# Casts of weights on VectorE during the attention, an early conversion dealt over more batches, and longer landing times for reloads in the planner

## The chip, the cores and the metric

One core of a Trainium2 chip runs the whole program. The metric is device time of one execution in microseconds; lower is better. The engines are PE (TensorE), ACT (ScalarE), DVE (VectorE), POOL (GpSimd) and SP (SyncE); SP and POOL issue the transfers.

## The reference

```python
scores = scale * np.matmul(q, k.transpose(0, 1, 3, 2)) - np.log(S)
attn = 1.0 / (1.0 + np.exp(-scores))          # sigmoid, no row sum
x = np.matmul(attn, v)                        # 4 batches x 12 heads, S 448, D 64
xn = x / np.sqrt(np.mean(x * x, -1) + 1e-06) * rms_g      # x: 1792 x 768
g, val = xn @ w_gate, xn @ w_val              # 768 -> 1536
y = (g / (1 + np.exp(-g)) * val) @ w_out      # 1536 -> 768
h = y @ w_in                                  # 768 -> 2048
out = (h - np.tanh(h)) @ w_out2               # 2048 -> 768
```

All of it is in float32 (x is first brought to 1792 rows of 768, the heads side by side).

## The kernel before

**Stages.** The attention runs over 4 batches, each of 6 pairs of heads: scores (L565, matmuls L576), sigmoids on ACT (L582, L583), the product with v (L596, matmuls L606), the copy of the result out of PSUM (pair_end, L613) and the sum of squares for the norm (x_end, L619: ACT squares in L621, DVE adds in L628). A batch's norm (L634) sums over channels on PE (L640), DVE reads these sums (L644), POOL takes the power (L646), and PE then writes over the same bank (whole_bank, L297), for which DVE must have read it. Then come the jobs: parts of w_gate ("Ag"), w_val ("Av"), w_out ("B"), w_in ("C") and the second w_out ("D"), each for two batches at a time, by schemes with seven products in place of eight (matmuls L881, L938) or plainly (L963). A product of float32 values is three passes over a high and a low part; a weight's high part is a cast (wt<-cv, L290) and its low part a difference (L371).

**Weights.** A raw piece is loaded by SP or POOL (load_raw, L334, L337; two slots). values32 (L353) makes float32 of it: a cast to zero (zero<-wt, L290) and a shift with an "or" on DVE (L360). For w_gate and w_val the conversion (conv, L436) goes on with sums (L452), splits, and stores to DRAM by SP (L434); for w_out (rows_early, L399) with sums (L420) and stores by POOL. 30 units of w_out's early conversion stand beside batches 0 and 1 of the attention, the loads and conversions of the first jobs of w_gate and w_val beside batch 3.

**Partial sums.** A job adds what it finished to sums kept in DRAM: POOL accumulates them (keep_sum, L748, L755). SP loads them again where a later job wants them: reload_sum (L675, L678) for the products with w_in, whose differences DVE takes in L691; reload_x (L670), prologue (L763) and set_units' get (L840) elsewhere. The epilogue's functions are L795 (silu), L798, L802 (tanh) and L803; additions of parts are L741 and L817.

**What sets the order.** Nothing runs while the code is read: each step is handed to a planner (Plan, L71) with the engines it may use and a modelled duration, what it reads and writes, and `after`, the modelled time from the end of an issue to the landing of a transfer (LAND; twice that for POOL). issue() takes, time after time, among the steps that could start within 300 ns of the soonest, the one of lowest rank (its place in the code plus `plan.later`), each on the engine that is done first, and at last writes out the program by modelled start. So a larger `after` puts what reads the data later and leaves the steps around it to move up. `copy` (L287) gives a cast or copy to ACT or DVE, whichever the planner finds sooner; with `act_copies` to ACT alone, which all jobs behind the attention have. `mixed` (L1050) deals lists of units evenly among the units of a batch's attention, with a rank some 60 places later. SP and POOL issue in the order of the program, and a waiting issue holds those behind it, as on every engine.

## Time and profile before

| | |
|---|---|
| Median of 3 runs | 1104.87 us (1102.76 to 1105.17) |
| The profiled execution | 1105.29 us |
| Span of its trace | 1103.5 us |
| Mean granted TensorE clock | 0.988 |
| PE busy | 1060.3 us (96%) |
| DVE, ACT, POOL busy | 773.2, 703.2, 138.8 us |

PE is busy nearly all the time, so the table says where little is left: in the stretches in which PE waits, and in those in which the throttle grants it less than the full clock. Where these are is read from the waits and the timelines. In a timeline row the bracket holds the idle time ahead of the instruction and what ended it; neighbours of one kind are one row with a count.

### The profile page before, as it was taken

Reading aid. Unit: us, or ns where it says so; the run is one execution under the profiler, and the core shown is the slowest. Engines: PE = TensorE matmul, PEld = TensorE weight load, DVE = VectorE, ACT = ScalarE, POOL = GpSimd, SP = SyncE. Lnnn points to the kernel's source line nnn. Section 1 sums busy time; section 2 is a strip of 40 time slices with the busy share of each in tenths; the row PEclk is TensorE's granted clock in tenths of the full one; section 3 lists DMA queues with packets and bytes.
Section 4 is the critical chain, followed back from the end, with each engine's and each line's share of the span. In section 5 each row is a group of like instructions: output and inputs, shape, how many; then the busy total and the mean of one; then the engine's idle time right before and its main releaser. Section 6 shows DMA issues by size and latency. Waiting matters only on the chain.

```text
span 1103.5 us, 15119 instructions
## 1 busy us (share of the span) xinstructions
PE 1060.3 (96%) x5148; PEld 877.4 (80%) x5148; DVE 773.2 (70%) x1212; ACT 703.2 (64%) x1263; POOL 138.8 (13%) x194
## 2 busy tenths in 40 slices
PE   8996999999999999999999799999999899999998
PEld 3332334999999889999999688989998789999997
DVE  3526571787687678786774585898886888677766
ACT  5763786567566546666666365686865776666652
POOL 2300000000003024111003012000303120003030
PEclk9997999999999999999999899999999999999999
DMA  8997454566866988969679639558958873649493
GB/s 311 343 336 225 129 145 159 189 230 202 310 209 172 313 301 161 333 235 314 237 259 270 187 87 226 188 192 306 225 193 212 248 177 107 201 158 209 121 190 125
DMA packets 105357, 240.92 MB, mean 218 GB/s; under 512 B 27072, under 2 KB 58304, under 8 KB 105280
## 3 DMA queue, kind: packets, MB, share of 16 engines
q1 hardware_dynamic: 81712, 174.91, 47.0%
q0 software_dynamic: 23264, 64.89, 24.3%
q8 instruction: 40, 0.66, 0.2%
q14 instruction: 37, 0.30, 0.1%
q10 hardware_dynamic: 304, 0.16, 0.1%
HBM read 149.08 MB, written 90.83 MB: 217 GB/s over the span
## 4 chain that ended last, share of the span: by engine, by line
PE 75%; issue 5%; DMA 5%; DVE 4%; POOL 2%; ACT 1%; SPq 0%; POOLq 0%; DVEq 0%; ACTq 0%
PE ps L938 39%; PE ps L881 23%; PE ps L963 4%; PE ps L606 4%; PE ps L576 4%; DMA wt<-in_w_out 2%; POOL out L755 2%; DMA unit<-sumB 1%; DVE wt L371 1%; DMA wAg<-cv 1%; ACT unit L290 1%; DVE unit L686 1%; ACT wt L290 1%; DVE unit L817 0%; DVE cv L360 0%
## 5 line engine op out<-in xcount | busy, mean ns | idle before, releaser
L938 PE MATMUL ps<-unit,wt 128*128 128x448 f32 x2520 | 525.7, 367 | 14.3 <-DVE unit L817 9.2
L938 PEld LDWEIGHTS ps<-unit,wt 128*128 128x128 f32 x2520 | 473.0, 188 | 60.4 <-DVE unit L817 10.8
L881 PE MATMUL ps<-unit,wt 128*128 128x448 f32 x1512 | 315.0, 366 | 3.4 <-DVE unit L686 1.5
L881 PEld LDWEIGHTS ps<-unit,wt 128*128 128x128 f32 x1512 | 283.3, 188 | 29.5 <-DVE unit L686 2.3
L371 DVE TENSOR_TENSOR wt<-cv,wt 128x768 fp32r<-128x768 f32 (+1 forms) x252 | 223.0, 891 | 99.8 <-ACT wt L290 97.8
L290 ACT COPY unit<-ps 128x448 f32<-128x448 f32 x297 | 156.2, 533 | 137.9 <-PE ps L938 54.4
L290 ACT CAST wt<-cv 128x768 fp32r<-128x768 f32 (+1 forms) x246 | 191.7, 784 | 79.1 <-PE ps L938 38.3
L290 ACT CAST unit<-unit 128x448 fp32r<-128x448 f32 x257 | 141.4, 567 | 49.8 <-DVE unit L798 19.7
L686 DVE TENSOR_TENSOR unit<-unit 128x448 fp32r<-128x448 f32 x252 | 152.4, 620 | 26.5 <-ACT unit L290 18.0
L817 DVE TENSOR_TENSOR unit<-ps,unit 128x448 f32<-128x448 f32 x168 | 103.6, 621 | 33.9 <-PE ps L938 20.8
L691 DVE TENSOR_TENSOR unit<-unit 128x448 f32<-128x448 f32 x144 | 88.1, 620 | 24.3 <-DMA unit<-sumB 18.2
L576 PE MATMUL ps<-wt 64*128 64x448 f32 (+1 forms) x384 | 82.7, 559 | 15.0 <-ACT unit L583 11.9
L583 ACT ACTIVATE unit<-ps 128x448 f32<-128x448 f32 (+1 forms) x192 | 86.1, 547 | 9.3 <-PE ps L576 9.3
L576 PEld LDWEIGHTS ps<-wt 64*128 64x128 f32 (+1 forms) x384 | 33.4, 176 | 60.5 <-issue 41.4
L606 PE MATMUL ps<-unit,cv 128*64 128x448 f32 (+1 forms) x384 | 79.3, 554 | 2.1 <-DMA cv<-in_vp 2.1
L360 DVE SCALAR_TENSOR_TENSOR cv<-wt,zero 128x768 uint32<-128x768 uint32 x68 | 64.9, 954 | 19.7 <-ACT zero L290 14.9
L290 ACT CAST zero<-wt 128x768 f16<-128x768 bf16 x56 | 60.2, 1075 | 21.5 <-DMA wt<-in_w_val 12.2
L755 POOL DMA_DIRECT2D sumB<-unit x48 | 41.4, 947 | 247.3 <-DVE unit L817 155.8
L606 PEld LDWEIGHTS ps<-unit,cv 128*64 128x64 f32 (+1 forms) x384 | 26.0, 139 | 52.3 <-issue 33.2
L963 PE MATMUL ps<-unit,wt 128*128 128x448 f32 x288 | 62.4, 374 | 2.8 <-ACT unit L290 1.9
L963 PEld LDWEIGHTS ps<-unit,wt 128*128 128x128 f32 x288 | 54.8, 192 | 9.4 <-ACT unit L290 2.7
L755 POOL DMA_DIRECT2D out<-unit x36 | 30.9, 937 | 180.5 <-DVE unit L817 164.1
(45 smaller groups left out, 402.3 us busy)
## 6 DMA issues: line engine op xcount, KB each, us to landing
wt<-in_w_out POOLq DMA_DIRECT2D x28, 768.0 KB, 7.9
cv<-wD SPq DMA_DIRECT2D x56, 384.0 KB, 5.4
cv<-wB SPq DMA_DIRECT2D x36, 384.0 KB, 5.5
wt<-in_w_in SPq DMA_DIRECT2D x16, 768.0 KB, 6.5
wC<-cv SPq DMA_DIRECT2D x32, 384.0 KB, 5.3
cv<-wC SPq DMA_DIRECT2D x32, 384.0 KB, 5.6
sumB<-unit POOLq DMA_DIRECT2D x48, 224.0 KB, 7.1
wD<-cv POOLq DMA_DIRECT2D x28, 384.0 KB, 6.1
```

Source lines behind the costliest of these rows:

```text
L290: add(engines, lambda e: (nc.scalar.copy if e == "ACT" else nc.vector.tensor_copy)(to(), of()), reads, writes)
L371: add({**dve(n, psum=False), **pool(n)}, lambda e: ENG[e].tensor_sub(lo(), of(), hi().bitcast(F32)), [*reads, *kh], [*kl])
L576: nc.tensor.matmul(ps[i, c].tile[:n, :S], lhsT=t.tile[rows, at:at + n], rhs=t.tile[rows, :S], start=True, stop=True)
L583: add(act(S, psum=True), lambda e: nc.scalar.activation(to.tile[at:at + n, :S], ps.tile[:n, :S], AF.Sigmoid, bias=-math.log(S), scale=1.0 ...
L606: nc.tensor.matmul(ps.tile[i * D:(i + 1) * D, :S], lhsT=v.tile[:n, c, i, :], rhs=a[c][i].tile[:n, :], start=(c == 0), stop=(c == 3))
L686: add({**pool(S), **dve(S, psum=False)}, lambda e: ENG[e].tensor_sub(t["l"].tile, of.tile, t["h"].tile.bitcast(F32)), [of["t"], kh], [kl])
L691: add({**dve(S, psum=False), **pool(S)}, lambda e: ENG[e].tensor_sub(t.tile, x.tile, y.tile), [x["t"], y["t"]], [t["t"]])
L755: add({"POOL": (1100, False)}, lambda e: nc.gpsimd.dma_start(out=d.tile, in_=t.tile, accum_op=ALU.add), [t["t"], d["t"]], [d["t"]], after= ...
L817: add(dve(S), lambda e: nc.vector.tensor_add(t.tile, ps.tile[:, :S], t.tile), [ps["t"], t["t"]], [t["t"]])
L881: nc.tensor.matmul(ps.tile[:, :S], lhsT=part(a), rhs=x[b].tile, start=n in (1, 5) and kp == 0 and q == 0, stop=kp == n_kp - 1 and q == 2, ...
L938: nc.tensor.matmul(ps.tile[:, :S], lhsT=part(a), rhs=x[b].tile, start=n in ((1, 2, 5) if opening else (1, 5)) and i == 0 and q == 0, stop= ...
L963: nc.tensor.matmul(ps.tile[:, :S], lhsT=wt, rhs=a[p].tile, start=start and i == 0, stop=stop and i == 2, skip_group_check=True)
```

## The change

It has three parts. `act_copies` becomes `copies_by`, which names an engine or none: the units of the early conversion of w_out, and those of the first two jobs' conversion beside batch 3, are wrapped by `by_dve`, so that their casts are DVE's; the copies of the attention itself stay free, and all jobs behind it have ACT as before. The 30 units of w_out are dealt 6, 12, 12 and 0 over the four batches where they were dealt 8 and 22 over the first two. And the planner counts 4500 ns to the landing of a load where it counted 3500 (POOL's: 9000 for 7000), and 10000 for the four kinds of reloads.

```diff
@@ -26,7 +26,6 @@
 SG = 4
 SPLIT = []
 EARLY = {"Ag": 0, "Av": 0, "C": 0}
-ACT_COPIES = "AgAvBCD"
 PLAIN_SETS = {("B", 0): (2,), ("D", 0): (), ("B", 1): (2,), ("D", 1): ()}
 
 NQK = S + 4 * P
@@ -42,9 +41,10 @@
 BEHIND, ROWS_BEHIND = 90, 90
 FIRST = 150
 HELD = 3
+ROWS_B = 20, 60, 100
 ROWS_BY = {"B": "POOL", "D": "POOL"}
 N_AGAIN = 4
-LAND = 3500
+LAND, FAR = 4500, 10000
 WINDOW = 500
 N_UNIT, N_MOE, N_RAW, N_WT, N_CV = 72, 40, 2, 8, 8
 AHEAD = 2
@@ -79,7 +79,7 @@
 
     def __init__(self, room):
         self.room, self.work, self.rank, self.later = room, [], [], 0
-        self.act_copies = False
+        self.copies_by = None
 
     def add(self, engines, run, reads=(), writes=(), stream=None, after=0):
 
@@ -285,8 +285,8 @@
         return {}
 
     def copy(engines, to, of, reads, writes):
-        if plan.act_copies:
-            engines = {"ACT": engines["ACT"]}
+        if plan.copies_by:
+            engines = {plan.copies_by: engines[plan.copies_by]}
         add(engines, lambda e: (nc.scalar.copy if e == "ACT" else nc.vector.tensor_copy)(to(), of()), reads, writes)
 
     g_sb = const.tile([P, KM], F32, name="g_sb")
@@ -670,12 +670,12 @@
     def reload_x(b, c):
         x = xs[b, c] = unit("xr")
         d = spilled.pop((b, c))
-        add({"SP": (650, False)}, lambda e: nc.sync.dma_start(out=x.tile, in_=d.tile), [d["t"]], [x[0], x[1]], after=LAND)
+        add({"SP": (650, False)}, lambda e: nc.sync.dma_start(out=x.tile, in_=d.tile), [d["t"]], [x[0], x[1]], after=FAR)
 
     def reload_sum(b, c):
         x = xg[b, c] = unit("xr")
         d = sums_t.pop(("B", b, c))
-        add({"SP": (650, False)}, lambda e: nc.sync.dma_start(out=x.tile, in_=d.tile), [d["t"]], [x["t"]], after=LAND)
+        add({"SP": (650, False)}, lambda e: nc.sync.dma_start(out=x.tile, in_=d.tile), [d["t"]], [x["t"]], after=FAR)
 
     right = {}
 
@@ -765,7 +765,7 @@
             ps = ps_t[ph, b, m] = bank("m2")
             if carried(ph, bs, s):
                 d, a = sums_t.pop((ph, b, m)), unit("accs")
-                add({"SP": (650, False)}, lambda e, a=a, d=d: nc.sync.dma_start(out=a.tile, in_=d.tile), [d["t"]], [a["t"]], after=LAND)
+                add({"SP": (650, False)}, lambda e, a=a, d=d: nc.sync.dma_start(out=a.tile, in_=d.tile), [d["t"]], [a["t"]], after=FAR)
                 seed(ps, a, False)
 
     def seed(to, of, psum):
@@ -841,7 +841,7 @@
             for mp in range(KM // 2):
                 a, d = unit("accs"), sums_t.pop((ph, bs[n], 2 * mp + m))
                 accs[m, n, mp] = a
-                add({"SP": (650, False)}, lambda e, a=a, d=d: nc.sync.dma_start(out=a.tile, in_=d.tile), [d["t"]], [a["t"]], after=LAND)
+                add({"SP": (650, False)}, lambda e, a=a, d=d: nc.sync.dma_start(out=a.tile, in_=d.tile), [d["t"]], [a["t"]], after=FAR)
 
         def done(n, mp):
             x, y, z = (banks.get((c, mp)) for c in "xyz")
@@ -1047,6 +1047,14 @@
                 units += part
         return units
 
+    def by_dve(units):
+        def run(u):
+            plan.copies_by = "DVE"
+            u()
+            plan.copies_by = None
+
+        return [lambda u=u: run(u) for u in units]
+
     def mixed(units, *others):
 
 
@@ -1063,13 +1071,14 @@
                     plan.later = 0
                     at[k] += 1
 
-    rows_b = [u for i in range(n_sets("B")) for u in rows_early("B", i)]
-    mixed(attn_units(0), rows_b[:8])
-    mixed(attn_units(1), [lambda: norm(0), lambda: spread_norm(0)], rows_b[8:])
-    mixed(attn_units(2), [lambda: norm(1), lambda: spread_norm(1), *x_units("A", BATCHES[0], False)])
+    rows_b = by_dve([u for i in range(n_sets("B")) for u in rows_early("B", i)])
+    at = [len(rows_b) * x // 100 for x in ROWS_B]
+    mixed(attn_units(0), rows_b[:at[0]])
+    mixed(attn_units(1), [lambda: norm(0), lambda: spread_norm(0)], rows_b[at[0]:at[1]])
+    mixed(attn_units(2), [lambda: norm(1), lambda: spread_norm(1), *x_units("A", BATCHES[0], False)], rows_b[at[1]:at[2]])
     for j in range(AHEAD):
         load(j)
-    mixed(attn_units(3), [lambda: norm(2)], [u for j in range(AHEAD) for u in (*conv(j), lambda j=j: load(j + AHEAD))])
+    mixed(attn_units(3), [lambda: norm(2)], [u for j in range(AHEAD) for u in (*by_dve(conv(j)), lambda j=j: load(j + AHEAD))], rows_b[at[2]:])
     norm(3)
 
 
@@ -1092,7 +1101,7 @@
 
     for j in range(len(jobs)):
         ahead = conv(j + AHEAD) + [lambda: load(j + 2 * AHEAD)]
-        plan.act_copies = jobs[j][0] in ACT_COPIES
+        plan.copies_by = "ACT"
         kind = kind_of(j)
         tight = is_tight(j)
         units = job_units(j, tight)
```

The order of the instructions shows the following. In names, a number tells one buffer from the next.

At the end of batch 1 SP issues loads of queries and keys (in_qkt), of values (in_vp, in_vt) and of raw weights. Before:

```order
L337 DMA wt_650<-in_w_gate 128x3072
L547 DMA cv_677<-in_vp 128x384
L547 DMA cv_677<-in_vp 32x128
L547 DMA cv_677<-in_vp 64x64 x2
L337 DMA wt_697<-in_w_gate 128x3072
L537 DMA wt_713<-in_qkt 128x896
L337 DMA wt_726<-in_w_val 128x3072
L434 DMA wAg_0_746<-cv_728 128x768
L547 DMA cv_759<-in_vp 128x384
L547 DMA cv_759<-in_vp 32x128
L547 DMA cv_759<-in_vp 64x64 x2
L537 DMA wt_780<-in_qkt 128x896
```

After:

```order
L547 DMA cv_674<-in_vp 128x384
L547 DMA cv_674<-in_vp 32x128
L547 DMA cv_674<-in_vp 64x64 x2
L537 DMA wt_698<-in_qkt 128x896
L337 DMA wt_702<-in_w_gate 128x3072
L547 DMA cv_722<-in_vp 128x384
L547 DMA cv_722<-in_vp 32x128
L547 DMA cv_722<-in_vp 64x64 x2
L537 DMA wt_745<-in_qkt 128x896
L337 DMA wt_749<-in_w_gate 128x3072
L337 DMA wt_775<-in_w_val 128x3072
```

Each load of w_gate now stands behind one or two loads of the attention more, and no store of a converted weight (wAg) stands between them; the next one comes behind the loads of in_vt.

On DVE at the same place, where wt_726 and wt_791 are raw pieces of w_val and L644 reads batch 0's norm. Before:

```order
L290 CAST zero_80<-wt_726 128x768
L360 SCALAR_TENSOR_TENSOR cv_829<-wt_726,zero_80 128x768
L290 CAST wt_843<-cv_728 128x768
L371 TENSOR_TENSOR wt_843<-cv_728,wt_843 128x768
L628 TENSOR_TENSOR unit_647<-unit_647,unit_846 128x448
L360 SCALAR_TENSOR_TENSOR cv_860<-wt_791,zero_80 128x768
L644 TENSOR_SCALAR ms_877<-ps_852 112x4
```

After, where wt_749 is the second raw piece of w_gate:

```order
L290 CAST zero_80<-wt_749 128x768
L360 SCALAR_TENSOR_TENSOR cv_831<-wt_749,zero_80 128x768
L628 TENSOR_TENSOR unit_632<-unit_632,unit_829 128x448
L452 TENSOR_TENSOR cv_850<-cv_831 128x3x128
L452 TENSOR_TENSOR cv_850<-cv_850,cv_796 128x3x128
L290 CAST wt_862<-cv_850 128x768
L371 TENSOR_TENSOR wt_862<-cv_850,wt_862 128x768
L644 TENSOR_SCALAR ms_879<-ps_855 112x4
```

Before, the cast of wt_791 (to zero) was ACT's and stood there among the sigmoids. Now all casts are DVE's, and L644 stands behind the whole conversion of w_gate's second piece, while w_val's come behind it.

On PE the norm itself moved by one group of matmuls. Before:

```order
L576 MATMUL ps<-wt 96x448 x4
L640 MATMUL ps<-ones,unit 112x1 x4
L576 MATMUL ps<-wt 128x448 x4
L297 LDWEIGHTS mark
L297 MATMUL ps<-mark 128x448
L606 MATMUL ps<-unit,cv 64x448 x8
L576 MATMUL ps<-wt 96x448 x4
```

After:

```order
L576 MATMUL ps<-wt 96x448 x4
L576 MATMUL ps<-wt 128x448 x4
L640 MATMUL ps<-ones,unit 112x1 x4
L606 MATMUL ps<-unit,cv 64x448 x8
L297 LDWEIGHTS mark
L297 MATMUL ps<-mark 128x448
L576 MATMUL ps<-wt 96x448 x4
```

L297, which writes the bank that L644 reads, now comes behind eight matmuls of L606 (sixteen in the trace's count) and not ahead of them.

Near 600 us DVE takes differences of reloaded sums (L691), and finishes products (L798, L817). Before:

```order
L691 TENSOR_TENSOR unit_5804<-unit_5761,unit_5754 128x448
L691 TENSOR_TENSOR unit_5816<-unit_5775,unit_5804 128x448
L371 TENSOR_TENSOR wt_5814<-cv_5625,wt_5814 128x768
L798 TENSOR_TENSOR unit_5451<-ps_5756,unit_5451 128x448
L371 TENSOR_TENSOR wt_5825<-cv_5702,wt_5825 128x384
L817 TENSOR_TENSOR unit_5809<-ps_5771,unit_5809 128x448
L741 TENSOR_TENSOR unit_5848<-unit_5451,unit_5837 128x448
L798 TENSOR_TENSOR unit_5480<-unit_5809,unit_5480 128x448
L817 TENSOR_TENSOR unit_5794<-ps_5739,unit_5794 128x448
```

After:

```order
L691 TENSOR_TENSOR unit_5817<-unit_5717,unit_5710 128x448
L798 TENSOR_TENSOR unit_5442<-ps_5759,unit_5442 128x448
L371 TENSOR_TENSOR wt_5812<-cv_5676,wt_5812 128x768
L741 TENSOR_TENSOR unit_5834<-unit_5442,unit_5829 128x448
L371 TENSOR_TENSOR wt_5822<-cv_5686,wt_5822 128x384
L817 TENSOR_TENSOR unit_5805<-ps_5772,unit_5805 128x448
L798 TENSOR_TENSOR unit_5474<-unit_5805,unit_5474 128x448
L817 TENSOR_TENSOR unit_5790<-ps_5742,unit_5790 128x448
```

One L691 is left ahead of L798 and L817; the other three come eight rows behind the last row shown. On SP the reloads of the first two sums come ahead of one load of w_in and one store that stood ahead of them.

At the end of the attention, ACT's order after (before, the first silu and its table load stand behind the last sigmoid):

```order
L583 ACTIVATE unit_1777<-ps_1750 128x448
L795 ACT_TABLE_LOAD
L795 ACTIVATE unit_1781<-unit_1681 128x448
L290 COPY unit_1795<-ps_1758 128x448
L621 ACTIVATE unit_1798<-unit_1795 128x448
L290 CAST zero_80<-wt_1664 128x768
L583 ACT_TABLE_LOAD
L583 ACTIVATE unit_1811<-ps_1783 96x448
L583 ACTIVATE unit_1815<-ps_1784 96x448
L583 ACTIVATE unit_1820<-ps_1785 96x448
```

One silu (L795) stands between two groups of sigmoids (L583), and with it two more table loads.


## Rows read from the trace of the kernel before

**Rows 1.** waits of TensorE, whole span: total us, times, longest

```profile
PE ps L576 <- ACT unit L583: 11.9, 2, 10.7
PE ps L938 <- DVE unit L817: 9.2, 3, 7.4
PE ps L963 <- ACT unit L290: 1.9, 2, 1.5
```

**Rows 2.** timeline of TensorE, attention: start, duration, instruction, [idle before <- releaser]

```profile
64.68 3.23 PE L606 MATMUL ps<-unit,cv 128*64 128x448 f32 x16 [2.14 <-DMA cv<-in_vp]
...
80.52 1.75 PE L576 MATMUL ps<-wt 64*96 64x448 f32 x8
...
95.50 1.86 PE L576 MATMUL ps<-wt 64*128 64x448 f32 x2 [10.65 <-ACT unit L583]
...
97.77 4.79 PE L606 MATMUL ps<-unit,cv 128*64 128x448 f32 x16
...
105.67 3.23 PE L606 MATMUL ps<-unit,cv 128*64 128x448 f32 x16
```

**Rows 3.** timeline of ScalarE, the same stretch

```profile
94.00 1.05 ACT L290 CAST zero<-wt 128x768 f16<-128x768 bf16 x1 [12.19 <-DMA wt<-in_w_val]
```

**Rows 4.** timeline of VectorE, the same stretch

```profile
80.60 0.60 DVE L290 CAST zero<-wt 128x768 f16<-128x768 bf16 x1 [13.35 <-DMA wt<-in_w_gate]
81.09 0.61 DVE L628 TENSOR_TENSOR unit<-unit 128x448 f32<-128x448 f32 x1
81.62 0.96 DVE L360 SCALAR_TENSOR_TENSOR cv<-wt,zero 128x768 uint32<-128x768 uint32 x1
82.62 0.56 DVE L290 CAST wt<-cv 128x768 fp32r<-128x768 f32 x1
83.21 0.96 DVE L371 TENSOR_TENSOR wt<-cv,wt 128x768 fp32r<-128x768 f32 x1
...
85.76 1.15 DVE L452 TENSOR_TENSOR cv<-cv 128x384 f32<-128x384 f32 x2
```

**Rows 5.** timeline of the queue of SyncE (SPq), the same stretch

```profile
73.45 0.52 SPq L337 DMA_DIRECT2D wt<-in_w_gate  x1
74.08 2.06 SPq L547 DMA_DIRECT2D cv<-in_vp  x4
...
85.48 0.53 SPq L537 DMA_DIRECT2D wt<-in_qkt  x1
86.11 0.38 SPq L337 DMA_DIRECT2D wt<-in_w_val  x1
```

**Rows 6.** landing times of the tile wt's transfers, 0 to 130 us

```profile
DMA to landing us min/median/max: 3.1/7.5/12.5
```

**Rows 7.** timeline of VectorE around 615 us

```profile
611.78 0.62 DVE L691 TENSOR_TENSOR unit<-unit 128x448 f32<-128x448 f32 x1 [8.14 <-DMA unit<-sumB]
614.95 0.63 DVE L691 TENSOR_TENSOR unit<-unit 128x448 f32<-128x448 f32 x1 [2.54 <-DMA unit<-sumB]
```

**Rows 8.** timeline of TensorE at 620 us; row of the chain at 959 us

```profile
619.63 25.75 PE L938 MATMUL ps<-unit,wt 128*128 128x448 f32 x117 [7.40 <-DVE unit L817]
...
959.24 21.90 PE ps L938 x108
```

**Rows 9.** SyncE's reloads near 600 us; their landing times, 560 to 680 us

```profile
597.50 3.01 SPq L678 DMA_DIRECT2D unit<-sumB  x4
...
DMA to landing us min/median/max: 2.8/8.4/14.7
```

**Rows 10.** windows: stretch; PE, PEld, DVE, ACT, POOL busy; PEclk, DMA share, GB/s

```profile
75.00:100.00 25.00, 14.35 (x61) 5.49 (x59) 15.79 (x28) 9.89 (x21) 1.03 (x1) 0.75 0.82 271
...
615.00:620.00 5.00, 0.37 (x1) 0.37 (x2) 4.97 (x9) 1.49 (x3) 0.00 (x0) 0.64 0.56 176
```

**Rows 11.** timeline of ScalarE at the end of the attention

```profile
195.60 1.28 ACT L795 ACT_TABLE_LOAD   x1
196.90 1.20 ACT L795 ACTIVATE unit<-unit 128x448 f32<-128x448 f32 x2
```

## The prediction

> **What bounds the kernel now.** I read the waits of TensorE first, then its timeline at the two longest, then the engines and the queue that those waits name. TensorE is busy for 96% of the span, so only its idle time and its time at a low clock can be won. Two waits stand out: 10.7 us of scores (L576) behind a sigmoid (L583), and 7.4 us of L938 behind an addition on VectorE (L817) [rows 1].
>
> The first is at the end of batch 1's attention. TensorE stops at 95.50 − 10.65 = 84.85 us [rows 2]. The sigmoids that should free its banks stand on ScalarE behind a cast that waits 12.19 us for a raw piece of w_val [rows 3]; SyncE issued that load at 86.11 [rows 5] and the cast could start at 94.00, so issue to use took 7.9 us. When TensorE resumes it is slow: two scores of L576 take 1.86 us [rows 2] where eight took 1.75, so 2 × 1.75 / 8 = 0.44 was due; the next sixteen L606 take 4.79 where others take 3.23. Together 1.42 + 1.56 = 3.0 us are lost; the window around it shows a granted clock of 0.75 [rows 10], a mix of the 1.2 and 2.4 GHz levels. This place costs 10.65 + 3.0 = **13.65 us**.
>
> The second is at 612 to 620 us. VectorE waits 8.14 and 2.54 us in L691 for reloaded sums [rows 7] that SyncE issued from 597.50 on and of which the slowest took 14.7 us to land [rows 9]; L817 stands behind them on VectorE, and TensorE idles 7.40 us [rows 8]. The 117 matmuls after that take 25.75 us, where 117 × 21.90 / 108 = 23.7 were due, so 2.0 go to the clock (0.64 granted in that window [rows 10]). It costs **9.4 us**.
>
> **The change part by part.** *The casts go to VectorE.* In the attention four casts to zero and two to wt change engine, 4 × 0.60 + 2 × 0.56 = 3.5 us more on VectorE [rows 4]. VectorE is busy 15.79 of the 25 us there [rows 10], so the time itself is hidden; uncovered it would be 3.5. ScalarE no longer holds a cast that waits for a weight until the attention's tail, so the 12.19 us wait leaves the sigmoids' queue. What is late next is on VectorE: L644 reads the norm's sums, TensorE's L297 writes over that bank afterwards, and in the new order L644 stands behind the whole conversion of the second w_gate piece. A waiting cast there holds L628, L452, L371 and L644, and then TensorE.
>
> When does that piece land? In the new order SyncE has, from the place of 73.45 us on [rows 5], a load of values (2.06), one of queries (0.53), the first w_gate (0.52), values again and queries again, before the second w_gate: 2.06 + 0.53 + 0.52 + 2.06 + 0.53 = 5.7, issue at 79.2. The store that waited for VectorE no longer stands ahead of it. The first w_gate piece went from issue at 73.45 [rows 5] to its cast at 80.60 [rows 4] in 7.15; so I put the second at 86.4. VectorE then does cast 0.60, L360 0.96, L628 0.61, two L452 1.15, cast 0.56, L371 0.96 [rows 4], 4.84 in all, and L644 runs at 91.2. TensorE, not stopped at 84.85, has the last two scores (0.44) and sixteen L606 (3.23) before L297 and reaches it at 88.5. Gap: 91.2 − 88.5 = 2.7.
>
> What does that gap cost in clock? Behind the idle time of 2.14 at 64.68 the sixteen L606 took 3.23 as elsewhere [rows 2], so nothing; behind 7.40 it was 2.0 [rows 8]. On the line between, 2.7 costs (2.7 − 2.14) / (7.40 − 2.14) × 2.0 = 0.2. So 13.65 becomes 2.9: **gain 10.7**. Bounds: 13.65, where the piece lands 2.7 us sooner and no gap is left; and 0, where the gap is again what it was. I take the value from the rows of this very load.
>
> *Loads of values.* With the weight loads behind them, the wait of 2.14 us for values at 64.68 [rows 2] may shrink: **gain 1**, between 0 and 2.14.
>
> *The early conversion of w_out.* 30 units go 6, 12, 12 beside batches 0 to 2 instead of 8 and 22 beside batches 0 and 1. That is only a rank for the planner, and the order shows little of it: the twelfth conversion stands on VectorE behind seven additions of squares (L628) where it stood behind five, some ten us later,, and is still in batch 1. POOL issues the same loads and stores. Its price is within the bounds above: **0**; if a store came to stand behind a later conversion, it would delay nothing before w_out is used, hundreds of us on.
>
> *Reloads planned 10 us long, other loads 4.5.* Near 600 us the sums' reloads move ahead on SyncE past one weight load and one store, and on VectorE three of the four L691 go some fifteen rows down; one L691 remains ahead of L798 and L817. If it starts with the first landing, as now at 611.78, its successors no longer wait for the second: L817 comes at least 614.95 − 611.78 = 3.2 earlier [rows 7]. The reloads' issue comes perhaps 4 us earlier too (one load and one store less, and the first pair first). With 3.2 + 4 the idle time of 7.40 is nearly gone, and its clock loss with it, in part. **Gain 7**, between 3.2 (landing unchanged) and 9.4 (all). Behind it the three L691 are next; the product that needs them comes later by these fifteen rows, and I count nothing.
>
> *The planner's other shifts.* From 360 to 410 us POOL issues four raws of the second w_out in a row instead of two and two. L963 waits 1.9 us in all for ScalarE [rows 1]. I take 0, from −2 to +4 (a queue of raws ahead of a store can delay what waits for it; of the two ends the first is the nearer).
>
> *Tables.* A silu (L795) now stands between two groups of sigmoids, so two more table loads: one took 1.28 [rows 11]. ScalarE has slack there and the matmuls of L938 now mixed between the last pairs fill TensorE: **cost 0.5**, between 0 and 2.6. The Trainium skill (ScalarE: Activation LUTs, What ACT_TABLE_LOAD costs) gives about 2.66 us per switch, since it adds a drain; here the next function starts at 196.90, right behind 195.60 + 1.28, so the trace shows no such drain.
>
> **Sum.** The profiled execution took 1105.29 us: its span of 1103.5 and 1.8 around it, and 0.4 over the median of 1104.87. 10.7 + 1 + 7 + 0 − 0.5 = 18.2, so 1105.3 − 18.2 = 1087.1, and 1086.7 on the median's side. Since the first term has more room below than above, I round up: **1088**.
>
> **The rivals.** *The wait only changes engines.* If the second w_gate lands after the longest of the loads, 12.5 us [rows 6], it is there at 91.7, L644 at 96.5, and the gap is 8.0 with (8.0 − 2.14) / 5.26 × 2.0 = 2.2 of clock: 10.2 of 13.65 remain, and the gain is 3.4. The time: 1105.3 − (3.4 + 1 + 7 − 0.5) = 1094.4, **1094**. For it: the DMA share of that window is 0.82 [rows 10]. Against: the piece before needed 7.15.
>
> *The sums land no earlier.* The DMA engines were full there, as 14.7 us to land say [rows 9]; an earlier issue may not help, and the waits pass to the three later L691. The third term is then 0 to 3.2: 1105.3 − (10.7 + 1 + 1.6 − 0.5) = 1092.5, **1093** (with the middle, 1.6).
>
> *Slower: the head of VectorE's queue.* The second w_gate is issued only behind the queries of 85.48 [rows 5], since SyncE must wait for free slots, and lands 12.5 later, at 98.0. L644 is at 102.8, the gap 14.3, and with clock 3.0 × 14.3 / 10.65 = 4.0 the place costs 18.3, 4.7 more than now. If the reloads gain nothing as well and the tables cost 0.5, it is 1105.3 + 5.2 = 1110.5, **1110**. It decides where the landing passes some 94 us with no gain at 612, or 100 with the whole of it.
>
> *The tables stand on TensorE's path.* Both loads would delay sigmoids that TensorE waits for: 2 × 1.28 = 2.56 instead of 0.5, **1090**. Against: they lie where L938 has work. By the Trainium skill's 2.66 (the same section) an estimate would be 5.3 instead of 2.56, 1093, with the rule that functions be grouped by table set; the trace's 1.28 bears out the lower.
>
> *The change does not do what it says.* The spread of w_out over three batches is such a case already; it carries no term, and is no rival in time.
>
> **How the numbers follow.** The forecast 0.58, the moved wait 0.17, the late sums 0.12, the slower one 0.08, the tables 0.05. Two runs of this kernel can be told apart by about 0.2%, 2.2 us. Faster by more than that: all of the forecast and the tables, 0.13 of the moved wait, 0.11 of the late sums, 0.87 in all. Within it: the rest of these two, where both shrink together, 0.05. Slower: 0.08. Range: from 1078, where both gaps vanish, the values come in time and the other shifts give their 2 (13.65 + 9.4 + 2.1 + 2 = 27.2), to 1102, where the moved wait and the late sums come together (3.4 + 1 − 0.5 = 3.9 is 1101.4).
>
> **What would show it.** Right: no sigmoid waits for a weight before 110 us; TensorE's idle time at L297 or the scores near 88 us is 1 to 5 us, with L644 behind a cast that waits for in_w_gate; L691 at 605 to 612 with one wait, and less than 3 us of idle time before L938 there. Wrong: L644 later than 95 us, an L691 wait of 8 us or more that TensorE repeats, or a new wait in the 200 to 1100 us that neither view above has. The forecast fails above all if SyncE's issues are held by slots, or if transfers land much later than 7 us.

## The result, and the profile after

The changed kernel takes 1089.2 us (median of 4 runs, 1087.35 to 1090.19) where the kernel before took 1104.0 in the same comparison: a ratio of 0.9864, 95% interval 0.9845 to 0.9883. The prediction was 1088 in a range of 1078 to 1102. The profiled execution, the fastest of the four, took 1087.35 with a span of 1085.6, so 17.9 us less span than before.

The waits of TensorE after (total us, times, longest) answer to [rows 1]:

```profile
PE ps L576 <- DMA wt<-in_qkt: 7.1, 2, 3.7
PE ps L938 <- ACT unit L290: 3.6, 3, 1.7
PE ps L297 <- DVE ms L644: 2.9, 1, 2.9
PE ps L938 <- DVE unit L817: 2.4, 3, 1.1
```

The 10.7 us behind the sigmoid and the 7.4 behind L817 are gone. In their place stand 2.9 us at L297 behind L644, which was forecast, and more for queries and keys at the very start, 7.1 us where it was 3.1 (2.69 and 0.41), which was not. TensorE's timeline of the attention answers to [rows 2]:

```profile
13.14 1.77 PE L576 MATMUL ps<-wt 64*128 64x448 f32 x8 [3.41 <-DMA wt<-in_qkt]
...
29.80 3.36 PE L576 MATMUL ps<-wt 64*128 64x448 f32 x8 [3.71 <-DMA wt<-in_qkt]
33.09 4.40 PE L606 MATMUL ps<-unit,cv 128*64 128x448 f32 x16
...
91.99 0.35 PE L297 MATMUL ps<-mark 128*128 128x448 bf16 x1 [2.90 <-DVE ms L644]
92.27 3.25 PE L576 MATMUL ps<-wt 64*96 64x448 f32 x16
95.45 3.23 PE L606 MATMUL ps<-unit,cv 128*64 128x448 f32 x16
```

VectorE, answering to [rows 4], shows what L644 waited for, and SyncE's queue, answering to [rows 5], when it was issued:

```profile
82.53 0.61 DVE L290 CAST zero<-wt 128x768 f16<-128x768 bf16 x1 [4.26 <-DMA wt<-in_w_gate]
...
87.02 0.62 DVE L290 CAST zero<-wt 128x768 f16<-128x768 bf16 x1 [1.19 <-DMA wt<-in_w_gate]
...
90.91 0.96 DVE L371 TENSOR_TENSOR wt<-cv,wt 128x768 fp32r<-128x768 f32 x1
91.79 0.15 DVE L644 TENSOR_SCALAR ms<-ps 112x4 f32<-112x4 f32 x1
```

```profile
75.91 0.51 SPq L337 DMA_DIRECT2D wt<-in_w_gate  x1
...
80.17 0.43 SPq L337 DMA_DIRECT2D wt<-in_w_gate  x1
```

VectorE's timeline near 590 us and then TensorE's, answering to [rows 7] and [rows 8]:

```profile
593.23 0.63 DVE L691 TENSOR_TENSOR unit<-unit 128x448 f32<-128x448 f32 x1 [7.63 <-DMA unit<-sumB]
```

```profile
597.75 3.97 PE L938 MATMUL ps<-unit,wt 128*128 128x448 f32 x18 [1.60 <-ACT unit L290]
602.22 24.00 PE L938 MATMUL ps<-unit,wt 128*128 128x448 f32 x117 [0.50 <-DVE unit L817]
```

One L691 still waits 7.63 us, but the second and the pair behind it no longer do, and TensorE loses 2.1 us where it lost 7.40. The 117 matmuls then take 24.00 us, not 25.75.

Where the 17.9 us came from can be read by the starts of the same TensorE instructions in both timelines:

| From one mark to the next (start in us before / after) | Gain in this stretch |
|---|---|
| start to the tenth group of sixteen L606 (77.36 / 78.64) | −1.3 |
| to the twelfth (105.67 / 95.45) | +11.5 |
| to the first 108 L881 (255.68 / 246.95) | −1.5 |
| to the second (332.71 / 323.87) | +0.1 |
| to 100 L963 (407.99 / 396.98) | +2.2 |
| to the next 108 L881 (498.56 / 486.00) | +1.55 |
| to the next (575.44 / 563.11) | −0.2 |
| to 100 L963 (654.84 / 635.67) | +6.8 |
| to two L881 (732.40 / 712.88) | +0.35 |
| to 86 L881 (1082.21 / 1064.17) | −1.5 |
| to the end of the span (1103.5 / 1085.6) | −0.1 |

### The profile page after: what moved, and what is told of

Its sections match the earlier page's. It is cut to its first block, busy times and chain, and to the rows that moved or that the text cites. A ratio compares the mean times of both kernels' runs of the same rounds, so it can differ in the third digit from the quotient of the medians.

```text
span 1085.6 us, 15124 instructions
## 1 busy us (share of the span) xinstructions
PE 1056.8 (97%) x5148; PEld 874.8 (81%) x5148; DVE 775.4 (71%) x1217; ACT 702.7 (65%) x1260; POOL 139.4 (13%) x194
## 4 chain that ended last, share of the span: by engine, by line
PE 73%; issue 10%; DMA 8%; DVE 3%; SPq 2%; POOL 2%; ACT 1%; POOLq 0%; DVEq 0%; ACTq 0%
PE ps L938 38%; PE ps L881 21%; PE ps L963 5%; PE ps L606 4%; PE ps L576 4%; DMA wt<-in_qkt 3%; POOL out L755 2%; DMA cv<-in_vp 2%; SPq L547 1%; DMA wt<-in_w_in 1%; DMA wt<-in_w_out 1%; DVE wt L371 1%; DMA out<-unit 1%; DVE unit L817 0%; DVE unit L686 0%
## 5 line engine op out<-in xcount | busy, mean ns | idle before, releaser
L938 PE MATMUL ps<-unit,wt 128*128 128x448 f32 x2520 | 524.8, 366 | 7.5 <-ACT unit L290 3.6
L938 PEld LDWEIGHTS ps<-unit,wt 128*128 128x128 f32 x2520 | 471.2, 188 | 56.1 <-ACT unit L290 6.4
L881 PE MATMUL ps<-unit,wt 128*128 128x448 f32 x1512 | 316.3, 367 | 4.0 <-DVE unit L686 1.6
L881 PEld LDWEIGHTS ps<-unit,wt 128*128 128x128 f32 x1512 | 284.8, 189 | 29.8 <-DVE unit L686 2.2
L290 ACT COPY unit<-ps 128x448 f32<-128x448 f32 x299 | 158.0, 534 | 138.9 <-PE ps L938 45.6
L290 ACT CAST wt<-cv 128x768 fp32r<-128x768 f32 (+1 forms) x244 | 190.3, 785 | 75.2 <-PE ps L938 32.0
L290 ACT CAST unit<-unit 128x448 fp32r<-128x448 f32 x256 | 140.9, 567 | 31.6 <-DVE unit L798 8.6
L817 DVE TENSOR_TENSOR unit<-ps,unit 128x448 f32<-128x448 f32 x168 | 103.5, 621 | 34.5 <-PE ps L938 17.1
L691 DVE TENSOR_TENSOR unit<-unit 128x448 f32<-128x448 f32 x144 | 87.7, 619 | 20.2 <-DMA unit<-sumB 14.0
L583 ACT ACTIVATE unit<-ps 128x448 f32<-128x448 f32 (+1 forms) x192 | 87.0, 546 | 18.7 <-PE ps L576 18.7
L576 PE MATMUL ps<-wt 64*128 64x448 f32 (+1 forms) x384 | 81.5, 558 | 7.1 <-DMA wt<-in_qkt 7.1
L606 PE MATMUL ps<-unit,cv 128*64 128x448 f32 (+1 forms) x384 | 79.1, 552 | 0.0
L576 PEld LDWEIGHTS ps<-wt 64*128 64x128 f32 (+1 forms) x384 | 32.6, 176 | 54.1 <-issue 47.5
L606 PEld LDWEIGHTS ps<-unit,cv 128*64 128x64 f32 (+1 forms) x384 | 25.6, 138 | 49.6 <-issue 32.4
L963 PE MATMUL ps<-unit,wt 128*128 128x448 f32 x288 | 60.9, 368 | 1.8 <-ACT unit L290 1.0
L290 ACT CAST zero<-wt 128x768 f16<-128x768 bf16 x52 | 56.0, 1076 | 9.9 <-DMA wt<-in_w_in 5.1
L963 PEld LDWEIGHTS ps<-unit,wt 128*128 128x128 f32 x288 | 53.6, 188 | 8.1 <-ACT unit L290 1.8
```

What stands on the lines that cost most here:

```text
L290: add(engines, lambda e: (nc.scalar.copy if e == "ACT" else nc.vector.tensor_copy)(to(), of()), reads, writes)
L576: nc.tensor.matmul(ps[i, c].tile[:n, :S], lhsT=t.tile[rows, at:at + n], rhs=t.tile[rows, :S], start=True, stop=True)
L583: add(act(S, psum=True), lambda e: nc.scalar.activation(to.tile[at:at + n, :S], ps.tile[:n, :S], AF.Sigmoid, bias=-math.log(S), scale=1.0 ...
L606: nc.tensor.matmul(ps.tile[i * D:(i + 1) * D, :S], lhsT=v.tile[:n, c, i, :], rhs=a[c][i].tile[:n, :], start=(c == 0), stop=(c == 3))
L691: add({**dve(S, psum=False), **pool(S)}, lambda e: ENG[e].tensor_sub(t.tile, x.tile, y.tile), [x["t"], y["t"]], [t["t"]])
L817: add(dve(S), lambda e: nc.vector.tensor_add(t.tile, ps.tile[:, :S], t.tile), [ps["t"], t["t"]], [t["t"]])
```

## The experiments

The first theory was the one of the prediction: the first place, at the end of batch 1, needs the casts on VectorE and SyncE's new order together; the second, near 600 us, is cured by the reloads' planned landing time. The rivals: the casts alone, or the planner's landing time for ordinary loads alone. All diffs below are against the changed kernel, if not said otherwise. With `ROWS_B = 27, 100, 100` the dealing is the old one (8 and 22 of 30 units), with 3500 the landing times are.

### One part at a time

**casts_only**

```diff
-ROWS_B = 20, 60, 100
+ROWS_B = 27, 100, 100
-LAND, FAR = 4500, 10000
+LAND, FAR = 3500, 3500
```

> Only the casts of the early conversions go to VectorE; the dealing (8, 22) and the planner's landing times (3500) are those of before. Theory 1 (the first place is cured by two things together: the cast must leave ScalarE, and SyncE must issue the w_gate loads ahead of the store that waits for VectorE): SyncE's order stays that of before, L644 stands on VectorE behind a cast of w_val whose load is issued near 86 us, so TensorE waits at L297 from about 85 to about 95 us; the second place is as before; 1101 to 1105 us. Theory 2 (taking the casts from ScalarE is enough for the first place): no wait over 4 us near 90 us; 1092 to 1095 us.

Measured: 1102.69 us, ratio to the kernel before 0.9987 (0.9966 to 1.0007), no difference that can be told. The wait only changed engines. TensorE, then VectorE:

```profile
92.17 0.53 PE L297 MATMUL ps<-mark 128*128 128x448 bf16 x1 [6.87 <-DVE ms L644]
```

```profile
78.82 0.62 DVE L290 CAST zero<-wt 128x768 f16<-128x768 bf16 x1 [10.53 <-DMA wt<-in_w_gate]
...
91.97 0.15 DVE L644 TENSOR_SCALAR ms<-ps 112x4 f32<-112x4 f32 x1
```

From 78.82 on VectorE never idles: L644 comes behind the conversions of three pieces and a cast of the fourth. So once the first piece of w_gate has landed it is work on VectorE that is waited for, and not the load of w_val, as the expectation had it.

**land_only**

```diff
-ROWS_B = 20, 60, 100
+ROWS_B = 27, 100, 100
-LAND, FAR = 4500, 10000
+LAND, FAR = 4500, 3500
-    rows_b = by_dve([u for i in range(n_sets("B")) for u in rows_early("B", i)])
+    rows_b = [u for i in range(n_sets("B")) for u in rows_early("B", i)]
...
-    ... (*by_dve(conv(j)), lambda j=j: load(j + AHEAD))], rows_b[at[2]:])
+    ... (*conv(j), lambda j=j: load(j + AHEAD))], rows_b[at[2]:])
```

> Only the modelled landing time of ordinary loads goes from 3500 to 4500 ns (reloads stay at 3500, casts are free, dealing 8 and 22). Its order on SyncE at the end of batch 1 and on VectorE near 600 us is that of the changed kernel. Theory 1: the cast of w_gate's or w_val's piece is still ScalarE's and holds the sigmoids, so 3 to 6 us of the first place remain, the second is cured by the order of L691: 1093 to 1097 us. Theory 2 (casts): the first place stays whole, 1097 to 1100. Theory 3 (the landing time alone makes the whole gain): 1087 to 1091 us.

Measured: 1092.83 us, ratio 0.9895 (0.9867 to 0.9922): 11.5 us, the largest of the single parts, and at the edge of what theory 1 expected. ScalarE's cast still waits, and TensorE too. The L290 that its row names is pair_end's copy, which VectorE had got and which came there, at 86.80, behind the conversion of another piece. ScalarE, then TensorE:

```profile
87.23 1.05 ACT L290 CAST zero<-wt 128x768 f16<-128x768 bf16 x1 [9.02 <-DMA wt<-in_w_gate]
```

```profile
87.47 3.58 PE L576 MATMUL ps<-wt 64*128 64x448 f32 x4 [4.08 <-DVE unit L290]
```

The second place is cured too: no wait behind L817 over 0.9 us is left, though one of 2.35 behind ScalarE has come.

**far_only** has `LAND, FAR = 3500, 10000`, with the old dealing and free casts as in land_only.

> Only the modelled landing time of the reloads goes from 3500 to 10000 ns. All four L691 near 600 us come behind L798 and L817; SyncE's order at the end of batch 1 is that of before. Theories 1 and 2: the second place is cured and the first stays, 1095 to 1098 us, with TensorE's wait of some 10 us near 95 us and none over 2 us near 612. Theory 3: the later L691 only hand the wait on, 1102 to 1105.

Measured: 1096.22 us, ratio 0.9917 (0.9888 to 0.9946). The first place is not cured. The second is, and wholly: the 171 L938 there run without a wait. TensorE at both places, then SyncE:

```profile
89.57 1.86 PE L576 MATMUL ps<-wt 64*128 64x448 f32 x2 [8.83 <-ACT unit L583]
...
593.67 34.88 PE L938 MATMUL ps<-unit,wt 128*128 128x448 f32 x171
```

```profile
590.14 3.01 SPq L678 DMA_DIRECT2D unit<-sumB  x4
```

The reloads were issued no earlier than before: 590.14 is 22.2 us behind the start of the 108 L881 ahead of them (567.92), where the kernel before had 22.1 (597.50 and 575.44). So L691's place behind L817 on VectorE is enough for the second place.

**deal_only** has the new dealing, 3500 for both landing times and free casts.

> Only the dealing of the early conversion of w_out changes (6, 12, 12 beside batches 0 to 2 for 8, 22). All theories: SyncE's order at the end of batch 1 and VectorE's near 600 us are those of before, so both places stay: 1102 to 1106 us. If the first 40 us have the wait of the changed kernel there (3.7 us and a low clock behind it), the dealing is its cause and the time is 1 to 4 us above before.

Measured: 1104.6 us, ratio 1.0009 (0.9990 to 1.0028). By itself the dealing does nothing to the time, as predicted. But it moves the norm on TensorE by one group of matmuls, as in the changed kernel (L640 behind sixteen L576, L297 behind the L606), and the wait of the first place now stands ahead of L640. The profile names no releaser; by the times it is again ScalarE's cast of w_val, with the sigmoids behind it. TensorE, then ScalarE:

```profile
93.02 1.62 PE L640 MATMUL ps<-ones,unit 128*112 128x1 f32 x8 [8.03 <-issue]
```

```profile
91.48 1.05 ACT L290 CAST zero<-wt 128x768 f16<-128x768 bf16 x1 [8.45 <-DMA wt<-in_w_val]
```

Its profile has 7.5 us of waits for queries at the start, casts_only 3.9, land_only 2.1 and far_only 1.7.

### All but one part

**all_but_casts** has free casts (the last two pieces of land_only's diff).

> The changed kernel with free casts in the attention (dealing and landing times as changed). SyncE's order is the changed one and L644 stands behind the same two L371 as in the changed kernel, while ScalarE has a cast to zero of a w_gate piece again. Theory 1 (place and cast both needed at the first place): 2 to 4 us slower than the changed kernel, 1091 to 1093, with a wait of sigmoids behind that cast. Theory 3 (the landing times make the gain, the engine of the casts matters only with the old order): within 2 us of the changed kernel, 1088 to 1091.

Measured: 1095.47 us, ratio to the kernel before 0.9906 (0.9881 to 0.9931): by the ratios some 5 us slower than the changed kernel (0.9906 against 0.9864; the intervals just touch), more than either theory gave. ScalarE's cast, then TensorE:

```profile
89.05 1.05 ACT L290 CAST zero<-wt 128x768 f16<-128x768 bf16 x1 [9.46 <-DMA wt<-in_w_gate]
```

```profile
89.26 1.86 PE L576 MATMUL ps<-wt 64*128 64x448 f32 x2 [4.82 <-DVE unit L290]
...
92.66 5.83 PE L606 MATMUL ps<-unit,cv 128*64 128x448 f32 x16
```

The cast holds ScalarE's sigmoids and, on VectorE, a copy out of PSUM (L290) stands behind another conversion. To the wait of 4.82 come sixteen L606 in 5.83 us where 3.23 are due. So the casts, worth nothing alone, are worth some 5 us beside the other parts.

**all_but_far** has `LAND, FAR = 4500, 4500`.

> The changed kernel with reloads planned at 4500 ns like the other loads. If the reloads' 10000 ns are what cures the second place: a wait of 5 us or more behind L817 near 605 us comes back, 1095 to 1098. If the ordinary landing time of 4500 already cures it: within 2 us of the changed kernel, 1088 to 1091.

Measured: 1090.68 us, ratio 0.9873 (0.9855 to 0.9892). Without the reloads' 10 us no wait behind L817 comes back: 4500 for every load is enough for that. TensorE waits 2.29 us behind ScalarE there (1.60 in the changed kernel). TensorE's wait at L297 in this profile:

```profile
91.60 0.53 PE L297 MATMUL ps<-mark 128*128 128x448 bf16 x1 [6.06 <-DVE ms L644]
```

Up to that point the order on every engine is that of the changed kernel, and there the wait was 2.90. L644 ran at nearly the same time (91.39, and 91.79 in the changed kernel); what differs is when TensorE came to L297, at 85.54 (91.60 − 6.06) and at 89.09 (91.99 − 2.90), above all because it had waited 3.5 us for queries at the start and not 7.1. So the wait at this place differs by 3 us between executions of one order, and what TensorE loses ahead of it is in part given back there.

**all_but_deal** has `ROWS_B = 27, 100, 100`.

> The changed kernel with the old dealing of the early conversion of w_out (8, 22). By the prediction the dealing costs and gives nothing: 1088 to 1091, and the wait of 3.7 us near 29 us may come or not. If the dealing (two units fewer in batch 0) causes that wait, it is gone here and the time 1083 to 1086.

Measured: 1091.46 us, ratio 0.9879 (0.9862 to 0.9895). Its interval overlaps that of the changed kernel; 2 us for the dealing is possible, not shown. The norm stands on TensorE where the kernel before had it, L297 ahead of the sixteen L606, and TensorE waits 4.17 us at L297. The early wait for queries is there (3.8 us), so the new dealing is not needed for it.

**all_but_land** has `LAND, FAR = 3500, 10000`.

> The changed kernel with ordinary loads planned at 3500 ns as before (casts on VectorE, dealing and the reloads' 10000 ns as changed). SyncE's order at the end of batch 1 is that of before, so L644 is on VectorE behind a run of conversions. If theory 1 holds (first place: casts and SyncE's order together), a wait of 5 to 9 us at L297 stays and the second place is cured by the reloads' term alone: 1093 to 1098 us. If the casts with the reloads' term were enough: 1088 to 1091.

Measured: 1092.30 us, ratio 0.9893 (0.9871 to 0.9915), just faster than theory 1 gave. The wait at L297 is there, TensorE:

```profile
94.00 0.53 PE L297 MATMUL ps<-mark 128*128 128x448 bf16 x1 [6.53 <-DVE ms L644]
```

### What is left of the first place

**norm_early**

```diff
-    mixed(attn_units(1), [lambda: norm(0), lambda: spread_norm(0)], rows_b[at[0]:at[1]])
+    mixed(attn_units(1), [lambda: norm(0), *[lambda: None] * 3, lambda: spread_norm(0)], rows_b[at[0]:at[1]])
```

> The changed kernel with batch 0's norm called after a fifth of batch 1's units and not after half of them, so that L644 stands on VectorE ahead of both pieces of w_gate. If what is left of the first place is L644 behind the conversion (theory 1): no wait at L297 over 0.5 us, 2 to 4 us faster than the changed kernel, 1085 to 1087. If it is only the first thing that meets a shortage of transfers there: another wait of 2 to 3 us takes its place within the next 10 us, and the time stays at 1088 to 1091.

Measured: **1083.26 us**, ratio to the kernel before 0.9799 (0.9776 to 0.9822). It beats both kernels: the changed kernel's interval lies wholly above, some 7 us away by the ratios, more than the 2 to 4 that theory 1 gave. The two profiled executions differ less, by 2.2 us of span, which the 2.90 at L297 covers; they are the fastest of the changed kernel's four runs and the slowest of norm_early's four. Whether the other executions of the changed kernel wait longer at L297, as all_but_far did, is not shown. L644 runs ahead of both waiting casts, and L297 and what follows wait for nothing. TensorE, then VectorE:

```profile
78.47 0.36 PE L297 MATMUL ps<-mark 128*128 128x448 bf16 x1
78.76 3.23 PE L606 MATMUL ps<-unit,cv 128*64 128x448 f32 x16
81.92 3.25 PE L576 MATMUL ps<-wt 64*96 64x448 f32 x16
```

```profile
76.94 0.15 DVE L644 TENSOR_SCALAR ms<-ps 112x4 f32<-112x4 f32 x1
...
82.45 0.61 DVE L290 CAST zero<-wt 128x768 f16<-128x768 bf16 x1 [3.30 <-DMA wt<-in_w_gate]
```

**casts_norm** is casts_only with the norm earlier still: seven empty units in place of three.

> The kernel of casts_only (casts on VectorE, nothing else) with batch 0's norm called after a ninth of batch 1's units, so that L644 stands behind the first w_gate piece's cast alone and no longer behind four conversions. If L644's place in VectorE's queue is what kept casts_only from gaining at the first place: the wait at L297 falls from 6.9 us to 1 to 3, 5 to 8 us faster than casts_only, 1094 to 1098. If SyncE's order must change too: another wait of 5 us or more follows before 100 us, and the time stays at 1101 to 1104.

Measured: 1101.53 us, ratio 0.9980 (0.9962 to 0.9999): not what theory 1 gave. L644 now stands behind one cast of w_gate, but TensorE reaches L297 earlier as well, at 70.7, while that piece comes at 77.4. VectorE, then TensorE:

```profile
77.41 0.60 DVE L290 CAST zero<-wt 128x768 f16<-128x768 bf16 x1 [11.01 <-DMA wt<-in_w_gate]
...
79.30 0.15 DVE L644 TENSOR_SCALAR ms<-ps 112x4 f32<-112x4 f32 x1
```

```profile
79.50 0.53 PE L297 MATMUL ps<-mark 128*128 128x448 bf16 x1 [8.83 <-DVE ms L644]
```

To be ahead of most of the conversion is no use; L644 has to be ahead of the first cast that waits.

**norm_only** is the kernel before with the norm as in casts_norm.

> The kernel before with the norm called as early as in casts_norm and nothing else. By theory 1 the sigmoids still stand behind ScalarE's cast of w_val, so TensorE's wait of 8 to 11 us behind L583 stays: 1102 to 1106 us. If L644 was what really ended the first place in the kernel before: no wait over 4 us near 95, 1092 to 1097.

Measured: 1101.99 us, ratio 0.9992 (0.9972 to 1.0011). The time is that of theory 1, the reason isn't: no long wait behind L583 came, but this one on TensorE:

```profile
81.52 0.53 PE L297 MATMUL ps<-mark 128*128 128x448 bf16 x1 [8.43 <-DVE ms L644]
```

With 8.4 us lost before, TensorE comes to the sigmoids late enough that ScalarE's next cast of a raw piece (88.36) starts without a wait. What stands first in line takes the wait.

**norm_far12** is norm_early with `LAND, FAR = 4500, 12000`.

> norm_early with the reloads planned at 12000 ns, by which the last L691 too comes behind L798 and L817 near 600 us. If that L691's wait (7.6 us on VectorE in the changed kernel) still costs TensorE the 1.6 us behind ScalarE and the 0.5 behind L817 there: 1 to 3 us faster than norm_early, 1080 to 1082. If those come from elsewhere: 1082 to 1085.

Measured: 1094.39 us, ratio 0.9924 (0.9898 to 0.9949), 11 us slower than norm_early by the medians and 14 by the ratios; the expectation was wrong. Near 600 us nothing was won: the wait behind ScalarE there is 1.60 us again, so it isn't the last L691's. ScalarE has there a cast that waits 5.01 us for a piece of w_in. And new waits come where norm_early has none. TensorE:

```profile
596.38 3.93 PE L938 MATMUL ps<-unit,wt 128*128 128x448 f32 x18 [1.60 <-ACT unit L290]
...
668.37 0.47 PE L938 MATMUL ps<-unit,wt 128*128 128x448 f32 x1 [2.16 <-ACT unit L290]
670.26 29.43 PE L938 MATMUL ps<-unit,wt 128*128 128x448 f32 x137 [1.42 <-DVE unit L686]
```

These make only part of the loss: the two profiled spans differ by 5.0, the medians by 11. The rest is open.

## Why the prediction was right, and where it was not

**First place: forecast 10.7, measured 11.5.** The chain held link by link. The second w_gate piece was forecast to be issued at 79.2 and cast at 86.4, L644 at 91.2 and TensorE's gap 2.7; they came at 80.17, 87.02, 91.79 and 2.90. The clock's 0.2 wasn't lost: the sixteen L576 behind the gap take 3.25, as elsewhere, at a granted clock of 1.00. Most of the 0.8 over the forecast lies in the kernel before, whose loss here was read too low: six L576 had taken the 1.77 us of eight, and L297 0.56 where it takes 0.35 after. TensorE before:

```profile
83.07 1.77 PE L576 MATMUL ps<-wt 64*128 64x448 f32 x6
...
97.29 0.56 PE L297 MATMUL ps<-mark 128*128 128x448 bf16 x1
```

That the gap came out at 2.90 is in part luck, since all_but_far had 6.06 with the same order. What the prediction left out is the weight of the parts. It named the casts first; the runs show that by themselves they hand the wait from ScalarE to VectorE (its first rival in small), and that the landing time of 4500 is worth most alone. With both, the wait is 2.90 or 6.06; without the landing time it is 6.53 (all_but_land), which one execution of each can't tell from 6.06, and without the casts 4.82, with 4.7 us more lost on slow matmuls behind it (all_but_casts). So that SyncE's order is needed beside the casts is not shown by these waits; the time without it is some 3 us longer by the ratios (0.9893 and 0.9864), and the intervals overlap. The norm's place in VectorE's queue, which it named as what is late next, was indeed what was left: norm_early takes it away.

**Second place: forecast 7, measured 6.8.** The effect was right: one L691 ahead, L817 free of the rest, and the reloads earlier. In the kernel before they were issued 22.1 us behind the start of the 108 L881 ahead of them (597.50 − 575.44), after 17.6 (580.69 − 563.11): 4.5 earlier where about 4 was the estimate. But this earlier issue, 4 of the prediction's 3.2 + 4, is not needed: far_only has none of it and no wait at all, with all four L691 behind L817. In the changed kernel, where one L691 stays ahead, no run parts the two. What TensorE still waits in the changed kernel, 1.60 us, comes behind a cast of ScalarE that waits for a piece of w_in:

```profile
596.26 1.05 ACT L290 CAST zero<-wt 128x768 f16<-128x768 bf16 x1 [5.06 <-DMA wt<-in_w_in]
```

far_only and all_but_land have no cast that waits there. Either planned time is enough to bring L817 ahead: far_only does it with 10000 for the reloads alone, all_but_far with 4500 for all loads. The parts overlap, so their single gains (11.5 for land_only, 8.1 for far_only) can't be added.

**Loads of values: forecast +1, measured −1.3.** This term failed. The 2.14 us at 64.68 are gone, yet the waits of 3.41 and 3.71 for queries at the start, and the slow L576 and L606 behind the second (3.36 for 1.77, 4.40 for 3.23), for which the prediction had no term, cost more. The kernel before lost less there: 2.69, 0.41 and 1.28 us, with one slow group:

```profile
12.73 3.19 PE L576 MATMUL ps<-wt 64*128 64x448 f32 x8 [2.69 <-DMA wt<-in_qkt]
```

The runs do not tie these waits to a part: totals of 1.7 to 7.5 us appear across kernels with and without each of them. What sets them stays open. Nor does this term stand apart from the first place: all_but_far, with less lost at the start, waited as much longer at L297.

**The dealing: forecast 0.** Measured: nothing alone; beside the rest some 2 us by the ratios, not told from 0. But "only a rank" was too little: where the norm's call was not moved, the runs with the new dealing have L297 behind the sixteen L606, those with the old one ahead of them (casts_only, land_only, far_only, all_but_deal). So the 3.23 us of L606 that the first term counted ahead of L297 come from the dealing.

**Other shifts: forecast 0, from −2 to +4; measured +3.7.** The table's 2.2 and 1.55: TensorE's four waits between 377 and 408 us (0.89, 1.32, 1.46, 0.39) became three (0.85, 0.62, 0.34), and the 100 L963 behind them take 20.70 and not 22.26, at a granted clock of 1.00 and not 0.92. Within its bounds, but mis-sized: I had no row that tied POOL's order to them.

**Tables: forecast −0.5; the stretch lost 1.5.** ScalarE has the two more table loads, three in all:

```profile
178.30 1.28 ACT L795 ACT_TABLE_LOAD   x1
179.60 0.58 ACT L795 ACTIVATE unit<-unit 128x448 f32<-128x448 f32 x1
...
182.50 1.28 ACT L583 ACT_TABLE_LOAD   x1
183.79 1.84 ACT L583 ACTIVATE unit<-ps 96x448 f32<-96x448 f32 x4
...
187.96 1.28 ACT L795 ACT_TABLE_LOAD   x1
```

Each takes 1.28 us and its function follows 0.01 to 0.02 us later, and TensorE has no wait behind them. The Trainium skill (ScalarE: Activation LUTs, What ACT_TABLE_LOAD costs), which the prediction weighed, adds a drain to each switch of the table set; this trace shows none here either. The 1.5 us go elsewhere, to a thing I had counted as free: the L938 dealt between the pairs.

```profile
144.76 0.87 PE L938 MATMUL ps<-unit,wt 128*128 128x448 f32 x3
145.56 1.72 PE L606 MATMUL ps<-unit,cv 96*64 96x448 f32 x8
...
156.23 1.48 PE L938 MATMUL ps<-unit,wt 128*128 128x448 f32 x6
157.64 1.77 PE L576 MATMUL ps<-wt 64*128 64x448 f32 x8
```

In an unbroken run one L938 takes 21.90 / 108 = 0.203 us [rows 8]. Here three hold TensorE from 144.76 to 145.56, 0.80 for 0.61, and six 1.41 for 1.22: some 0.19 us more for each group. There are six such groups between the pairs where there was one. The groups of L576 and L606 that they split take longer too: two times eight L576 take 1.68 and 1.71 us from start to start where sixteen take 3.18. Between the two marks of the table, all L576 and L606 together take 79.1 us where they took 78.1, and all L938 65.9 where they took 65.4, which is the 1.5. This is read from the rows and wasn't tried by itself.

**Not foreseen:** −1.5 between 732 and 1082 us. A little more waiting near 840 to 850, and then 89 L881 in 20.02 us at a granted clock of 0.91 where the kernel before had them in 18.30 at 1.00. all_but_deal, all_but_land and norm_early have 19.8 to 20.0 there, all other kernels 18.3 to 18.5. These four are the kernels that have both the casts on VectorE and the reloads at 10000; with one of the two, or with 12000, it does not appear. How the two act together there is open, and each kernel has one profile only.

**Sum.** 11.5 + 6.8 + 3.7 against −1.3, −1.5 and −1.5, with 0.1 from the four small stretches, makes 17.9 before rounding, where 18.2 was forecast. In this pair of profiles the two large terms were right to a microsecond; that the total is right to 0.3 is luck in the small ones. Against the medians the gain is 14.8, since the profiled execution of before lay above its median and that of after below. So the typical gain was forecast 3.4 us too large, and no single profile tells in which term. The time came within 1.2 us all the same, because the forecast started from 1105.3, 1.3 above the median of 1104.0, and rounded up by 0.9: luck again.

## What to carry to other kernels

An instruction that waits for a transfer holds its whole queue. Moving it to another engine gained nothing here while something that TensorE needs stood behind it there; so ask of the new queue what short, urgent instruction (here 0.15 us of L644) is behind it, and put that ahead of the first one that waits, not merely ahead of most. And a planner's landing time is an order, not a fact: 1 us longer for every ordinary load was worth 11 us here, and 2 us longer still for the reloads lost as much, for reasons only in part found.

## What the hardware showed that I had not expected

- The clock behind an idle stretch could not be read off its length here. In the changed kernel, behind 3.41 us (13.14) eight L576 took 1.77 at a granted clock of 1.00 (2.4 GHz), nothing lost; behind 3.71 (29.80) they took 3.36 at 0.50 (1.2 GHz), and the L606 after them 4.40 at 0.72. Behind the 2.90 at L297 the clock stayed at 1.00. In the kernel before, 2.69 us (12.73) were enough for 3.19 at 0.54. The prediction's straight line between 2.14 and 7.40 us has no support in these rows.
- The same order of instructions gave waits of 2.90 and 6.06 us at the same L297 in two executions, with L644 at 91.79 and 91.39: the wait ended at nearly the same time however early TensorE came. One profile sizes such a place to some 3 us only.
- Short groups of 128x128 matmuls between others with 64 rows or columns took about 0.19 us each above their rate in a long run, and a group of sixteen L576 split by one some 0.2 us more than a whole one (1.68 and 1.71 for 3.18).
